# A third landing tile for the q and k loads, with the mask setup's tiles moved into a weight block's place

## Chip, cores, metric

The kernel runs on one NeuronCore of one Trainium2 chip. Its metric is device time in microseconds (us) of one execution, the median of three. Five engines run side by side, each through its own instruction stream in a fixed order: PE (TensorE, matmuls), DVE (VectorE), ACT (ScalarE), POOL (GpSimd) and SP (SyncE, which here only starts transfers). They wait for one another through semaphores. Transfers between device memory and the on-chip memory (SBUF) are started from SP and from ACT.

## The reference, cut to what matters

```python
# attention: batch 4, heads 8, sequence 768, head size 64; 4 sink columns, window 128
scores = q @ k^T / sqrt(64)
keep   = (pos_k < n_sink) | ((0 <= pos_q - pos_k) & (pos_q - pos_k < window))
a      = softmax(where(keep, scores, -1e9))
x      = (a @ v), heads side by side        # 3072 tokens x 512
# feed-forward
h = x @ w_in                                # 512 -> 2048
g = max(h, 0) + alpha * min(h, 0)
out = g @ w_out                             # 2048 -> 512
```

All of it is float32 at the interface.

## The kernel before

**Tiling.** The 3072 tokens are cut into 12 chunks `c` of 256 queries. For a chunk, `attention(c)` goes over 8 heads; each head has two units of 128 queries (`unit`), which see only a window of 260 keys and sinks. Then come the transposition of the weights and the product with v (`av_split`, `av`, `av_two`), which leaves the chunk's x as a rounded part `xh` and a remainder `xl`. The feed-forward part takes 16 weight blocks `f` of 128 hidden units: `gemm1(c, f)` makes h on PE (L863), ACT and DVE make g and its two parts `gh` and `gl` (L867 to L870), and `gemm2(c, f)` adds their product to the chunk's output (L898 to L901).

**Loads of the heads.** One transfer brings q and k of a head (`load_head`, L441) into a tile of the kind `stage`, 128 x 648 floats (324 KB); there are two such tiles. For the chunks 0 and 1 (`SPLIT`) one transfer brings a pair of heads, and PE reads the tile itself (L585), so it comes free when the second unit of the pair is done. From chunk 2 on ACT and DVE make a rounded copy `kq` of it (`prep_head`: L558 and L559 on ACT, L560 and L562 on DVE), and the tile comes free with L562. `next_load()` places the load of a later head in the program wherever a head begins. The first chunk's four pairs do not use `stage`: they land in `early`, tiles lent from places of SBUF that weight blocks 15 and 14 will take much later (`lend`; the tag `w15`, `w14`). The first values v land in the place of block 13 the same way.

**Weights.** A weight block arrives as 1 MB of raw 64-bit numbers (`load_weights`, tile `wraw`) and is turned into a high and a low float32 part by `convert_weights`: L382 on ACT first, then DVE steps (L386, L387, L396), L401 on ACT or DVE and L404 on DVE. Blocks 0 to 3 are loaded from SP, 4 to 15 from ACT's queue (L372). A block may be loaded no sooner than the conversion of the block four before has begun.

**Mask setup.** In the first 6 us POOL and DVE build the masks of the window: index tiles `geo` and `geof`, 128 x 2 x 260 each (L503, L504), are written by POOL (L520 to L526) and read by DVE (L524 to L537). After that they are not used.

**What sets the order.** `Plan` is a list scheduler that runs while the program is built. Each step is an `op` with an engine, a cost in us from a small table and the values that it reads and writes; values of a kind (`stage`, `kq`, `wa`, PSUM banks and so on) share that kind's tiles in the order of their making. `draw` plays all engines forward with these costs, and `issue` writes each engine's instructions in the order found. It also keeps a model of the transfers: an op with `nbytes` is held back while the modelled transfer queue is more than `BACKLOG` = 4 us ahead. So a changed number of tiles can change the order on any engine. Up to 28 us, `fill` adds matmuls of no use (`idle`, L1057) where PE would stand still.

Of the kernel before, what the change touches and what calls it, by code (L numbers as in the profile page):

```python
# [9 lines left out]
F32 = mybir.dt.float32  # L10
# [5 lines left out]
I32 = mybir.dt.int32  # L16
# [3 lines left out]
P = 128  # L20
# [3 lines left out]
WIN = 2 * P + NS  # L24
QC = 2 * P
KC = 3 * P + 2 * NS
CPB = S // QC
NCHUNK = B * CPB
NF = DF // P
# [49 lines left out]
class Plan:  # L79
# [20 lines left out]
    def held(self, tile_):  # L100
        v = Value(None)
        v.at = tile_
        return v
# [218 lines left out]
def program(ctx, tc, qk, pairs, vp, vq, vs, w, par, out):  # L322
    nc = tc.nc
    const = ctx.enter_context(tc.tile_pool(name="const", bufs=1))
    fast = ctx.enter_context(ExitStack())
    pool = fast.enter_context(tc.tile_pool(name="main", bufs=1))
# [8 lines left out]
    def several(name, n, shape, dtype):  # L335
        plan.kind(name, [pool.tile(shape, dtype, name=f"{name}{i}") for i in range(n)])
# [2 lines left out]
    plan.kind("swap", [scratch.tile([4, P, P], F32, name=f"swap{i}") for i in range(2)])  # L339
    plan.kind("turns", [scratch.tile([4, P, 2 * 32], F32, name=f"turns{i}") for i in range(2)])  # L340
    trid = held(scratch.tile([P, 2, P], F32, name="trid"))
    several("stage", 2, [P, QC + KC], F32)
    several("kq", 2, [P, KC + 2 * QC], F32R)
    several("v", 2, [P, 3, 2, D], F32)
    several("pt_", 3, [P, 2, WIN], F32)
# [62 lines left out]
    stage, vtile, vst = {}, {}, {}  # L408

    lent = {}  # L410

    def lend(f, shape, count):
        box = {}

        def part(i):
            if "tile" not in box:
                box["tile"] = const.tile([P, count, *shape], F32, tag=f"w{f}", name="lent")
            return box["tile"][:, i]
        out_ = []
        for i in range(count):  # L420
            v = held(None)
            v.bind, v.box = lambda i=i: part(i), box
            out_.append(v)
        lent[f] = out_
        return out_

    early = lend(NF - 1, [QC + KC], 3) + lend(NF - 2, [QC + KC], 1)
    early_v = lend(NF - 3, [3, 2, D], 4)

    def bound(v):  # L430
# [38 lines left out]
    V = {}  # L469

    def setup(engine, cost, run, reads=(), writes=()):
        for x in (*reads, *writes):
            V.setdefault(x, held(x))
        return op(engine, cost, run, reads=[V[x] for x in reads], writes=[V[x] for x in writes])
# [26 lines left out]
    load_head(1, 1)  # L501
    load_head(1, 3)

    geo = pool.tile([P, 2, WIN], I32, name="geo")  # L504
    geof = pool.tile([P, 2, WIN], F32, name="geof")
    rel, relf = geo[:, 0, :2 * P], geof[:, 0, :2 * P]
    srel, srelf, past = [t.rearrange("p (a i s) -> p a i s", a=2, i=3) for t in (geo[:, 1, :6 * NS], geof[:, 1, :6 * NS], geof[:, 1, 6 * NS:12 * NS])]
    past = past[:, 0]
# [32 lines left out]
    setup("POOL", 0.3, lambda: nc.gpsimd.affine_select(tri[:, 1], tri[:, 1], pattern=[[1, P]], compare_op=ALU.is_ge, fill=0.0, base=0, channel_multiplier=-1), (), ("tri",))  # L541
    setup("DVE", 0.07, lambda: nc.vector.memset(fm, 0.0), (), ("fm",))

    xh, xl, prep, comb, sink, ptile_, sums, rinv, nms, wt = {}, {}, {}, {}, {}, {}, {}, {}, {}, {}

    def bank(c, n, tag):
# [528 lines left out]
    with tc.If(bad != 0):  # L1075
# [3 lines left out]
        with tc.For_i(0, B, 1) as b:  # L1079
            for cc in range(CPB):  # L1080
                x = general(nc, gen, ptile, cc, b, qk5, vp5, nsink, window, ident)
# [167 lines left out]
```

## Time and profile before

| | |
|---|---|
| median of 3 runs | 680.22 us (680.05 to 680.34) |
| the profiled execution | 680.29 us, of which the span from first to last instruction is 678.3 us |
| granted TensorE clock, mean | 0.995 |
| q and k loads (324 KB each) | 4 into lent tiles, 4 pairs and 80 heads into `stage` |
| weight loads (1 MB each) | 4 from SP, 12 from ACT |

The profile's views name a group of instructions by line, engine, operation and tiles (`pt<-pt,nm`: written tile, read tiles). "Busy" counts the time in which an engine works on an instruction. An idle stretch is put down to the event that ended it, its releaser: "<-DVE nm L607 1.2" reads "1.2 us of waiting, ended by line 607 on DVE". SPq and ACTq are the instructions that start transfers, and "to landing" is the time from a start to the moment at which the data may be used. Times within the profile are counted from the start of the span.

### The profile page before, as it was taken

How to read it: one execution, taken by the hardware profiler on the slowest of the kernel's cores; microseconds unless marked ns; L12 is line 12 of the kernel's file. 1: busy time of each engine (PE TensorE's matmuls, PEld its weight loads, DVE VectorE, ACT ScalarE, POOL GpSimd, SP SyncE). 2: the span in 40 equal slices, each digit the busy share in tenths (PEclk: the TensorE clock that was granted, in tenths of full speed). 3: DMA queues.
4: the chain of work that ended last, by engine and by line, in shares of the span. 5: the costliest groups of instructions: out<-in, count | busy, mean ns of one | idle time of the engine just before them, and what ended most of it. 6: DMA issues, size and time to landing. Idle time of an engine off the chain costs nothing.

```text
span 678.3 us, 13313 instructions
## 1 busy us (share of the span) xinstructions
PE 664.5 (98%) x4534; PEld 581.7 (86%) x4534; DVE 533.8 (79%) x1795; ACT 402.4 (59%) x1084; POOL 35.6 (5%) x115
## 2 busy tenths in 40 slices
PE   9989999999999999999999999999999999999996
PEld 4568898988889889898988988988988988988995
DVE  6999999968968967976986985895995995995331
ACT  6989987836637637536646545655654663743332
POOL 2110000001000000001000000000000000100000
PEclk9989999999999999999999999999999999999998
DMA  8765541434433544443443552543542453431001
GB/s 311 270 217 215 194 164 42 124 92 152 124 119 107 148 115 130 137 141 106 145 141 96 139 150 87 156 125 90 166 144 68 154 150 86 149 94 47 32 2 35
DMA packets 64732, 87.56 MB, mean 129 GB/s; under 512 B 13968, under 2 KB 41104, under 8 KB 64656
## 3 DMA queue, kind: packets, MB, share of 16 engines
q1 hardware_dynamic: 61104, 73.53, 36.0%
q10 hardware_dynamic: 3552, 13.11, 5.6%
q8 instruction: 37, 0.61, 0.4%
q14 instruction: 39, 0.32, 0.2%
HBM read 68.40 MB, written 18.22 MB: 128 GB/s over the span
## 4 chain that ended last, share of the span: by engine, by line
PE 82%; DVE 9%; ACT 5%; issue 2%; DMA 2%; POOL 0%; ACTq 0%; SPq 0%; DVEq 0%
PE bank L863 34%; PE bank L898 12%; PE bank L900 11%; PE bank L901 11%; PE bank L768 6%; PE bank L594 3%; PE bank L595 3%; DVE wa L396 2%; ACT pt L611 1%; DVE w L404 1%; DVE wa L394 1%; ACT wa L382 1%; DVE g L868 1%; DVE gl L870 1%; PE bank L838 1%
## 5 line engine op out<-in xcount | busy, mean ns | idle before, releaser
L863 PE MATMUL bank<-xh,w 128*128 128x256 f32 x1536 | 307.1, 281 | 1.5 <-DVE g L868 1.3
L863 PEld LDWEIGHTS bank<-xh,w 128*128 128x128 f32 x1536 | 251.1, 189 | 8.8 <-DVE g L868 1.8
L863 PE MATMUL bank<-xl,w 128*128 128x256 f32 x768 | 215.0, 280 | 0.0
L867 ACT ACTIVATE g<-bank,param 128x256 f32<-128x256 f32 x192 | 90.0, 471 | 114.9 <-PE bank L863 113.1
L900 PE MATMUL bank<-w,gh 128*128 128x512 f32 x382 | 151.9, 398 | 0.0
L901 PE MATMUL bank<-w,gh 128*128 128x512 f32 x382 | 149.9, 392 | 0.0
L863 PEld LDWEIGHTS bank<-xl,w 128*128 128x128 f32 x768 | 145.0, 189 | 5.2
L869 ACT CAST gh<-g 128x256 fp32r<-128x256 f32 x192 | 77.4, 404 | 89.0 <-DVE g L868 88.8
L868 DVE TENSOR_TENSOR g<-bank,g 128x256 f32<-128x256 f32 x192 | 80.1, 418 | 62.9 <-ACT g L867 62.5
L898 PE MATMUL bank<-w,gl 128*128 128x512 f32 x382 | 120.4, 397 | 0.0
L611 ACT ACTIVATE pt<-pt,nm 128x260 f32<-128x260 f32 (+1 forms) x192 | 94.2, 491 | 28.6 <-DVE nm L607 27.4
L870 DVE TENSOR_TENSOR gl<-g,gh 128x256 fp32r<-128x256 f32 x192 | 80.7, 422 | 25.0 <-ACT gh L869 22.0
L607 DVE CUSTOM_DVE_ANT_0 pt<-bank,masks 128x260 f32<-128x260 f32 (+1 forms) x192 | 74.5, 399 | 12.6 <-PE bank L595 9.1
L898 PEld LDWEIGHTS bank<-w,gl 128*128 128x128 f32 x382 | 69.5, 188 | 16.0 <-issue 2.2
L900 PEld LDWEIGHTS bank<-w,gh 128*128 128x128 f32 x382 | 71.9, 188 | 8.4 <-ACT kq L558 0.2
L901 PEld LDWEIGHTS bank<-w,gh 128*128 128x128 f32 x382 | 71.9, 188 | 8.4
L752 DVE TENSOR_TENSOR wa<-comb,tri 128x256 f32<-128x256 f32 x144 | 51.4, 419 | 2.1 <-DMA comb<-swap 1.9
L560 DVE TENSOR_TENSOR kq<-stage,kq 64x392 fp32r<-64x392 f32 x80 | 45.3, 566 | 5.7 <-ACT kq L558 3.3
L656 POOL TENSOR_TENSOR sink<-pt,ri 128x8 f32<-128x8 f32 x80 | 22.4, 280 | 494.4 <-DVE ri L641 205.3
L558 ACT CAST kq<-stage 128x392 fp32r<-128x392 f32 x80 | 41.4, 517 | 11.0 <-PE bank L595 6.3
L594 PE MATMUL bank<-kq 128*128 128x260 f32 (+1 forms) x160 | 45.2, 283 | 1.0 <-DVE nm L607 0.8
L595 PE MATMUL bank<-kq 128*128 128x260 f32 (+1 forms) x160 | 45.0, 281 | 0.1
(126 smaller groups left out, 685.6 us busy)
## 6 DMA issues: line engine op xcount, KB each, us to landing
stage<-qk SPq DMA_DIRECT2D x80, 324.0 KB, 3.0
wraw<-w ACTq DMA_DIRECT2D x12, 1024.0 KB, 5.3
swap<-comb SPq DMA_DIRECT2D x36, 256.0 KB, 2.0
comb<-swap SPq DMA_DIRECT2D x36, 256.0 KB, 3.1
v<-vq SPq DMA_DIRECT2D x36, 192.0 KB, 2.5
out_dram<-ob SPq DMA_DIRECT2D x22, 256.0 KB, 2.2
wraw<-w SPq DMA_DIRECT2D x4, 1024.0 KB, 12.3
turns<-comb SPq DMA_DIRECT2D x18, 128.0 KB, 3.3
```

Source lines behind the costliest of these rows:

```text
L594: nc.tensor.matmul(s[:, w0], qh()[:, qs], ks()[:, kw], start=True, stop=False)
L595: nc.tensor.matmul(s[:, w0], ql()[:, qs], ks()[:, kw], start=False, stop=True)
L607: op("DVE", dve(n), lambda: nc.vector.tensor_tensor_reduce(out=pt.at[:, u, w0], in0=s.at[:, w0], in1=masks[:, i, w0], scale=-0.125, scalar ...
L611: op("ACT", exp(n), lambda: nc.scalar.activation(pt.at[:, u, w0], pt.at[:, u, w0], AF.Exp, bias=nm.at[:, h, u:u + 1], scale=-1.0, accum_ou ...
L863: nc.tensor.matmul(h(), fin.at[:, 0, part, ks], rhs.at[:, kt], start=(kt == 0 and n == 0), stop=(kt == KT - 1 and n == 2))
L867: op("ACT", act(QC, True), lambda: nc.scalar.activation(g.at, h(), AF.Copy, scale=alt[:, f:f + 1]), reads=[bk, known("param")], writes=[g])
L868: op("DVE", dve(QC), lambda: nc.vector.tensor_tensor(g.at, h(), g.at, ALU.max), reads=[bk], writes=[g])
L869: op("ACT", cast(QC), lambda: nc.scalar.copy(gh.at, g.at), reads=[g], writes=[gh])
L870: op("DVE", dve(QC), lambda: nc.vector.tensor_tensor(gl.at, g.at, gh.at.bitcast(F32), ALU.subtract), reads=[g, gh], writes=[gl])
L898: nc.tensor.matmul(o2[j].at, gl.at[:, js], fin.at[:, 1, 0], start=False, stop=(f == NF - 1))
L900: nc.tensor.matmul(o2[j].at, gh.at[:, js], fin.at[:, 1, 0], start=(f == 0), stop=False)
L901: nc.tensor.matmul(o2[j].at, gh.at[:, js], fin.at[:, 1, 1], start=False, stop=False)
```

## The change

`stage` has three tiles in place of two. `geo` and `geof` are no tiles of their own any more: they lie behind the fourth early pair in the tile that is lent from weight block 14's place. The load of block 14 has the five mask values in the list of things that it must wait for.

```diff
-    several("stage", 2, [P, QC + KC], F32)
+    several("stage", 3, [P, QC + KC], F32)
...
     early = lend(NF - 1, [QC + KC], 3) + lend(NF - 2, [QC + KC], 1)
+    shared = const.tile([P, 1, QC + KC + 4 * WIN], F32, tag=f"w{NF - 2}", name="lent")
+    early[3].box["tile"] = shared[:, :, :QC + KC]
     early_v = lend(NF - 3, [3, 2, D], 4)
...
-    geo = pool.tile([P, 2, WIN], I32, name="geo")
-    geof = pool.tile([P, 2, WIN], F32, name="geof")
+    spare = shared[:, 0, QC + KC:].rearrange("p (n a x) -> p n a x", n=2, a=2)
+    geo, geof = spare[:, 0].bitcast(I32), spare[:, 1]
...
+    lent[NF - 2] += [V[x] for x in ("rel", "srel", "relf", "srelf", "past")]
```

The diff puts three lines in, so that a line number behind them is 2 or 3 higher after the change (L441 becomes L443, L607 becomes L610, L863 becomes L866). What it does to the order of the instructions shows at three places.

**SP, some 11 to 40 us into the span.** The rows start transfers; a name's first number is the buffer (`stage0`, `stage1`, `stage2`), and `pairs` and `qk` are the loads of two heads and of one. Before:

```order
L372 DMA wraw_324<-w 128x2x1024
L456 DMA v0_83<-vp 128x384
L456 DMA v1_84<-vp 128x384
L710 DMA trid_78<-tri_133 128x256
L441 DMA stage0_79<-pairs 128x648
L441 DMA stage1_80<-pairs 128x648
L441 DMA stage0_79<-qk 128x648
L456 DMA v0_83<-vp 128x384
```

After:

```order
L372 DMA wraw_323<-w 128x2x1024
L443 DMA stage2_81<-pairs 128x648
L458 DMA v0_84<-vp 128x384
L458 DMA v1_85<-vp 128x384
L713 DMA trid_78<-tri_133 128x256
L443 DMA stage0_79<-pairs 128x648
L443 DMA stage1_80<-qk 128x648
L443 DMA stage2_81<-qk 128x648
L458 DMA v0_84<-vp 128x384
```

The third pair of chunk 1 moves up behind weight block 3 and ahead of the first v loads. From there on each slot of a `stage` load stays where it was in SP's order and carries the next pair or head. The pattern holds to the last chunk, in which one slot is left over and falls away.

**ACT, 25 to 38 us.** `wraw` with a new number each time is weight block 4, 5, 6 (`wraw_380`, `432`, `472` before; `430`, `470`, `479` after), and the last row of each piece is the first step on block 4. Before:

```order
L707 CAST sinkT0_108<-bank2_66 128x256
L372 DMA wraw_380<-w 128x2x1024
L401 CAST w1_383<-wa1_93 128x2x512
...
L611 ACTIVATE pt_0_85,sm1_99<-pt_0_85,nm1_97 128x260
L372 DMA wraw_432<-w 128x2x1024
L635 COPY comb0_88<-bank2_66 128x512
...
L372 DMA wraw_472<-w 128x2x1024
L611 ACTIVATE pt_1_86,sm1_99<-pt_1_86,nm1_97 128x260
L611 ACTIVATE pt_2_87,sm1_99<-pt_2_87,nm1_97 128x260
L382 ACTIVATE wa0_92,size_124<-wraw_380 128x1024
```

After:

```order
L614 ACTIVATE pt_0_86,sm1_100<-pt_0_86,nm1_98 128x260
L372 DMA wraw_430<-w 128x2x1024
L638 COPY comb0_89<-bank2_66 128x512
...
L372 DMA wraw_470<-w 128x2x1024
L614 ACTIVATE pt_1_87,sm1_100<-pt_1_87,nm1_98 128x260
L614 ACTIVATE pt_2_88,sm1_100<-pt_2_88,nm1_98 128x260
L372 DMA wraw_479<-w 128x2x1024
L382 ACTIVATE wa0_93,size_125<-wraw_430 128x1024
```

The first of the three starts falls away; block 4 starts in the slot that block 5 had, block 5 in that of block 6, and block 6 directly ahead of the first step on block 4. All of ACT's other rows up to the last chunk's attention are in the order that they had.

**PE and DVE, in the last chunk's attention (near 600 us).** PE's score products (L594, L595, from then L597, L598) of one unit move from behind the ninth of a block's twelve `gemm1` products to ahead of the first. On DVE, before:

```order
L870 TENSOR_TENSOR gl2_123<-g1_117,gh2_120 128x256
L560 TENSOR_TENSOR kq1_82<-stage1_80,kq1_82 64x392
L752 TENSOR_TENSOR wa1_93<-comb1_89,tri_133 128x256 x4
L562 TENSOR_TENSOR kq1_82<-stage1_80,kq1_82 128x256
L868 TENSOR_TENSOR g0_116<-bank4_68,g0_116 128x256
L607 ISA pt_0_85,nm1_97<-bank0_64,masks_131 128x260
```

After:

```order
L873 TENSOR_TENSOR gl2_124<-g1_118,gh2_121 128x256
L610 ISA pt_0_86,nm1_98<-bank0_64,masks_131 128x260
L755 TENSOR_TENSOR wa1_94<-comb1_90,tri_133 128x256 x4
L563 TENSOR_TENSOR kq1_83<-stage2_81,kq1_83 64x392
L565 TENSOR_TENSOR kq1_83<-stage2_81,kq1_83 128x256
L871 TENSOR_TENSOR g0_117<-bank4_68,g0_117 128x256
```

One evacuation of a score bank (L607) moves four rows up, and two more steps of the same chunk change places behind it. Outside of these few dozen rows PE, DVE and POOL run the same instructions in the same order before and after.

## The prediction

> **What bounds the kernel now.** I read the page's first part, then the busy time by stretch, then who PE waits for.
>
> ```profile
> PE 664.5 (98%) x4534; PEld 581.7 (86%) x4534; DVE 533.8 (79%) x1795; ACT 402.4 (59%) x1084; POOL 35.6 (5%) x115
> ...
> 20.00:130.00 110.00, 105.65 (x696) 88.95 (x696) 107.48 (x254) 96.53 (x220) 6.39 (x17) 0.98 0.52 174
> 130.00:620.00 490.00, 488.29 (x3399) 437.39 (x3400) 396.87 (x1445) 274.91 (x790) 24.77 (x76) 1.00 0.42 124
> ```
>
> The two rows of stretches give, behind the length, the busy us of PE, PE's weight loads, DVE, ACT and POOL, then the granted clock, the share of the transfer engines and GB/s. There are two regimes. From 20 to 130 us, while weights are converted, DVE is busy 107.48 of 110 us: it leaves 110 - 107.48 = 2.5 us in which it could go faster. From 130 to 620 us PE is busy 488.3 of 490 us, and its order and number of matmuls are the kernel's arithmetic. The whole span's DVE share of 79% is a mean over both and hides the first.
>
> A third tile for loads can only help where something waits for a load. PE's longest waits and the only one on a transfer, and then what stood ahead of the engines when they turned to a `stage` tile (any access to it, PE, ACT or DVE):
>
> ```profile
> PE bank L585 <- DVE nm L607: 2.2, 2, 1.2
> PE bank L863 <- DVE g L868: 1.3, 2, 0.7
> ...
> PE bank L594 <- DVE nm L607: 0.8, 1, 0.8
> ...
> PE bank L585 <- DMA lent<-pairs: 0.3, 1, 0.3
> ...
> its engine sat idle before it (us, times) until:
>   PE bank L595: 6.3, 16
>   DVE nm L607: 4.9, 4
>   ACT kq L558: 3.3, 12
>   ACT xh L848: 3.2, 6
>   issue: 1.1, 4
>   ACT gh L869: 1.0, 5
> ```
>
> Each row is waiter, releaser, us in total, times, longest (the second list: releaser, us, times). The only load that PE waited for is that of a lent tile at the start, 0.3 us, and that load is the same after the change. In the second list every releaser is an engine; no transfer is among them. So the loads into the two tiles are always there in time already.
>
> How early they are is seen best where they are tightest, in the start, when weights fill the queues:
>
> ```profile
> 28.89 0.33 SPq L441 DMA_DIRECT2D stage<-pairs  x1
> stage<-pairs SPq DMA_DIRECT2D x1, 324.0 KB, 2.9
> 34.07 0.33 SPq L441 DMA_DIRECT2D stage<-pairs  x1
> 35.80 1.05 PE L585 MATMUL bank<-stage 64*128 64x260 f32 x4 [1.21 <-DVE nm L607]
> ```
>
> The load of chunk 1's third pair starts at 28.89 and lands 2.9 us later (the row of transfers for that start), at 31.8; PE reads it at 35.80, 4.0 us after. The 1.21 us ahead of that matmul are a score bank's, not the load's.
>
> **The loads after the change, step by step.** In SP's order every `stage` slot stays, from 28.89 us on, and carries the next load. Before, the load of head m waits until head m-2 has left its tile (two tiles). After, that slot loads head m+1 into the third tile on, so it waits for head m+1-3 = m-2: the same event. SP is therefore held as long as before at each slot, and the transfers that transpose the attention weights (`swap`, `comb`, `turns`) and v loads queued behind it on SP start when they did. Their bytes are the same at the same times. 80 heads and 4 pairs are loaded in either case. Gain: 0 us, because a load that is a head earlier replaces one that nobody waited for. Where the last slot falls away, near 590 us, the transfer behind it on SP can start a little sooner; PE waits for none of these in that stretch, so 0 us too.
>
> The one extra early load: the third pair goes out at the place of the first v load, in a stretch with full transfer engines.
>
> ```profile
> 12.15 1.38 SPq L456 DMA_DIRECT2D v<-vp  x2
> 10.00:20.00 10.00, 9.42 (x63) 5.07 (x61) 8.41 (x25) 9.37 (x27) 1.48 (x4) 1.00 1.04 403
> 23.00:26.00 3.00, 2.85 (x19) 1.77 (x18) 2.85 (x7) 2.94 (x8) 1.04 (x2) 1.00 0.16 59
> v<-vp SPq DMA_DIRECT2D x1, 192.0 KB, 12.6
> 43.55 1.63 PE L768 MATMUL bank<-comb,v 128*64 128x256 f32 x18
> ```
>
> At 403 GB/s its 324 KB (331,776 bytes) take 0.82 us. Weight block 3 is ahead of it in the queue and does not move. The two v loads and the mask transfer behind it land 0.82 us later; v landed at 12.15 + 12.6 = 24.8 and is read at 43.55, so 18 us cover it. The backlog runs into the nearly empty 23 to 26 us (share 0.16). Cost: 0; without that cover it would be 0.82 us.
>
> **The weight loads on ACT** are the only part with a thin cover.
>
> ```profile
> 25.36 0.44 ACTq L372 DMA_DIRECT2D wraw<-w  x1
> 30.00 0.39 ACTq L372 DMA_DIRECT2D wraw<-w  x1
> 33.69 0.37 ACTq L372 DMA_DIRECT2D wraw<-w  x1
> 37.26 1.13 ACT L382 ACTIVATE wa<-wraw 128x1024 f32<-128x1024 f32 x1 [0.38 <-DVE w L404]
> 44.73 1.17 ACT L382 ACTIVATE wa<-wraw 128x1024 f32<-128x1024 f32 x1
> ...
> wraw<-w ACTq DMA_DIRECT2D x1, 1024.0 KB, 5.0
> wraw<-w ACTq DMA_DIRECT2D x1, 1024.0 KB, 6.1
> wraw<-w ACTq DMA_DIRECT2D x1, 1024.0 KB, 5.6
> DMA to landing us min/median/max: 4.8/5.8/13.2
> ```
>
> The first three rows are the starts of blocks 4, 5 and 6, the next two ACT's first steps on blocks 4 and 5; then the three blocks' times to landing in that order, and the spread over all 16 weight loads. After the change block 4 starts where block 5 did, at 30.00. Block 5's row is the measurement of that slot, with the same load from SP (28.89) just ahead of it: 6.1 us, so block 4 lands at 36.1. ACT turns to it at 37.26. **The cover shrinks from 37.26 - 30.4 = 6.9 us to 1.2 us, and holds.** Block 5 starts at 33.69 and lands near 39.3 (5.6 us), 5.4 us ahead of its step at 44.73. Block 6 starts just ahead of 37.26 and lands near 43.4 (6.1 us), and ACT's step on it comes later still than that on block 5. What the start itself costs ACT is bounded by its row of 0.44 us: that much could be won at 25.36, and 0.44 - 0.38 = 0.06 us lost ahead of 37.26, where ACT idles 0.38 us. Both lie in the stretch that DVE sets, so I take 0.
>
> Why block 5 took 6.1 us and block 4 only 5.0: the Trainium skill, page "DMA: Bandwidth & Descriptors", section "Queues, rings and completion order", says that each transfer engine takes turns between the queues of SP and ACT, and that a completion signal lands only after all earlier writes of that engine, in any queue. By it a weight load behind an SP load of 324 KB ends up to 0.8 us later, as an estimate from that page and the rate of 403 GB/s; the trace's difference of 1.1 us is near it. As block 4's new slot is measured with that neighbour, the sum by the rule is the same; it says only that a further SP load in front would eat most of the cover.
>
> **The mask tiles** cost nothing: same POOL and DVE instructions in the same order with the same tiles waited for, done by 5.4 us, while block 14's load starts at 86.98:
>
> ```profile
> 4.35 1.07 DVE L537 TENSOR_SCALAR masks<-geof,pv 128x128 bf16<-128x128 f32 x5
> 86.98 0.37 ACTq L372 DMA_DIRECT2D wraw<-w  x1
> ```
>
> **The last chunk's reordering.**
>
> ```profile
> 600.16 0.28 PE L863 MATMUL bank<-xh,w 128*128 128x256 f32 x1
> 601.22 0.28 PE L594 MATMUL bank<-kq 128*128 128x260 f32 x1
> 598.59 1.43 DVE L752 TENSOR_TENSOR wa<-comb,tri 128x256 f32<-128x256 f32 x4
> 600.61 0.42 DVE L607 CUSTOM_DVE_ANT_0 pt<-bank,masks 128x260 f32<-128x260 f32 x1
> ```
>
> The score products of 601.22 go to 600.16. They need the score bank that the evacuation of 600.61 frees; that now comes ahead of the four mask products of 598.59 and is over by 598.59 + 0.42 = 599.0, so PE finds the bank free more than 1 us before. DVE's steps on g behind it move back by one or two evacuations, at most 2 x 0.42 = 0.8 us. `gemm2` uses them two blocks later (`LAG`), a dozen products and more. Cost 0; 0.8 us if that cover were gone.
>
> **The sum**: 0 + 0 + 0 + 0 on the profiled execution's 680.29 us, which lies 0.07 above the median of 680.22. Forecast 680.2.
>
> **Rivals.**
>
> *Slower: block 4 comes too late.* ACT runs in order, so if the load takes longer than 37.26 - 30.00 = 7.3 us, all behind L382 slips: the copies that feed PE's products, and through them DVE, in the stretch where DVE has 2.5 us of slack in 110. The price is the time to landing less 7.3 us; with the longest landing among the weight rows, 13.2 us, it is 5.9 us: 686.1. For it speaks that this cover is the thinnest and that rows of 12 to 13 us exist. Against it: those are SP's loads under the full queue of the first 23 us, and from 25 us on the three rows are 5.0 to 6.1. It needs 8.7 us or more to show at 0.2%. The clock could add to it:
>
> ```profile
> 34.00:39.00 5.00, 2.76 (x15) 1.84 (x16) 4.81 (x16) 4.24 (x11) 0.96 (x2) 1.00 0.97 346
> 39.00:44.00 5.00, 4.99 (x27) 4.33 (x27) 4.94 (x11) 5.00 (x15) 1.09 (x2) 0.66 0.27 72
> ```
>
> After a stretch with PE busy 2.76 of 5 us the granted clock is 0.66, and PE is then busy throughout. The Trainium skill, page "TensorE: Matmul & The Clock Gate", section on the HAM clock gate, has the clock halved after an idle window of about 3.4 us; the trace agrees in kind. By it a late block would prolong the slow stretch by about one window, an estimate of 1.7 us more.
>
> *Faster: the loads did matter.* A wait for several things is put to the last; if the 2.2 us of L585 at 35.80 and 38.46 were the third pair's load in truth, they would go, with the dip of the clock behind them. 2.2 us off is 678.0, and DVE's 2.5 us is the most that can be had at all, 677.7. Against it: the load landed 4.0 us before, and DVE's bank evacuation ended right at the wait's end.
>
> *The cover at 600 us is missing*: 0.8 us, 681.0, still within 0.2%.
>
> **How the numbers follow.** 0.2% is 1.4 us, about what a measurement of this kernel can tell from no change. Forecast 0.86, and with the cover missing at 600 us 0.02, both within 0.2%; block 4 late by enough to show 0.07; faster 0.05. Within the forecast, PE's two waits after 130 us (0.8 and 0.7 us, the row of L594, and the longest in that of L863) hang on small shifts of DVE and may go or grow: about 0.8 either way, and the 0.8 upwards from the last chunk is no more than that. So 679.4 to 681.1 holds more than 8 in 10; the rivals' ends lie outside.
>
> **What would show it.** Right: in the profile after, no transfer among the releasers at `stage`; starts of `stage` loads at the same times as before from 28.9 us on; ACT's L382 at 37.3 without a wait on `wraw`; block 4's load started near 30.0 and landed by 36.2; the same waits of PE. Wrong: a wait of ACT for `wraw<-w` near 37 us, more idle DVE than 2.5 us up to 130 us, a longer dip of the clock, or a wait of DVE for `comb<-swap` that grew from the loads' new neighbours.

## The result, and the profile after

| | before | after |
|---|---|---|
| median | 680.13 us (679.99 to 680.34) | 683.9 us (683.67 to 684.3) |
| after / before, 95% interval | | 1.0056 [1.0044, 1.0069] |
| profiled execution, span | 680.29, 678.3 us | 683.68, 682.0 us |
| PE busy in the span | 664.5 us | 669.7 us |

The kernel is 3.8 us slower, and PE is busy 5.2 us longer with the same matmuls. The profile after, its busy line and the busy time by stretch (behind the length: PE, PE's weight loads, DVE, ACT, POOL, then granted clock, transfer share, GB/s):

```profile
PE 669.7 (98%) x4532; PEld 583.8 (86%) x4534; DVE 534.1 (78%) x1795; ACT 404.8 (59%) x1084; POOL 36.2 (5%) x115
```

```profile
39.00:44.00 5.00, 4.99 (x48) 4.05 (x46) 4.93 (x11) 5.00 (x16) 1.08 (x2) 1.00 0.74 293
...
130.00:620.00 490.00, 489.13 (x3374) 436.58 (x3373) 394.58 (x1437) 275.27 (x785) 25.05 (x76) 1.00 0.41 123
```

The last row is the one to read beside the prediction's. In the same 490 us, at the same clock of 1.00, PE was busy 488.29 us with 3399 matmuls before and is busy 489.13 us with 3374 now: 143.7 ns for one before, 145.0 ns after. PE has no new gap; it gets 25 fewer matmuls done in a stretch in which it never rests, and 25 x 145 ns are 3.6 us. The first row shows that the loss comes in spite of a better start: there the granted clock was 0.66 before and is 1.00 now, and at 65 us the steps that make g start 0.84 us earlier than before. From about 100 us on the lead melts away evenly. The better start is not the change's doing. Among the kernels tried below, e2 has three `stage` tiles and e6 has two, and in this stretch they show, in this order:

```profile
39.00:44.00 5.00, 4.99 (x29) 4.31 (x29) 4.95 (x11) 5.00 (x16) 1.10 (x2) 0.66 0.66 263
```

```profile
39.00:44.00 5.00, 4.99 (x48) 4.00 (x46) 4.94 (x11) 5.00 (x16) 1.09 (x2) 1.00 0.25 70
```

The same in steps from one matmul's start to the next one's, averaged over all neighbours within a product between 160 and 590 us, without the slowest twentieth: 116.0 ns before and 118.0 after in the first product (L863 before, L866 after), 230.7 and 232.7 in the second. Times the matmuls in 130 to 620 us (1763 and 882 before) that is 1763 x 2.0 + 882 x 2.05 ns = 5.3 us. Less the 0.84 us of the better start, and less 0.8 us because PE's wait at L594 (near 443 us) is gone, this is about the 3.7 us between the spans.

What the prediction had looked at is as it said. Who PE waits for now, and what stood ahead of the engines when they turned to a `stage` tile:

```profile
PE bank L588 <- DVE nm L610: 2.2, 2, 1.2
PE bank L866 <- DVE g L871: 1.2, 2, 0.7
PE bank L1060 <- DVE fm L544: 1.0, 1, 1.0
PE bank L633 <- ACT pt L614: 0.7, 3, 0.3
PE bank L805 <- ACT sinkT L710: 0.6, 1, 0.6
```

```profile
its engine sat idle before it (us, times) until:
  PE bank L598: 5.8, 15
  DVE nm L610: 5.2, 5
  ACT xh L851: 3.9, 7
  ACT kq L561: 3.5, 15
  ACT gh L872: 1.4, 5
  issue: 0.7, 3
```

No load is among them, and no wait has grown by what the kernel lost. At the start, weight block 4's load and ACT's first step on it:

```profile
30.23 0.43 ACTq L372 DMA_DIRECT2D wraw<-w  x1
...
37.49 1.12 ACT L382 ACTIVATE wa<-wraw 128x1024 f32<-128x1024 f32 x1 [0.39 <-DVE w L404]
```

```profile
wraw<-w ACTq DMA_DIRECT2D x1, 1024.0 KB, 5.5
```

The load starts at 30.23 and lands at 35.7, 1.8 us ahead of the step at 37.49, which waited only for DVE.

So the same instructions of one engine became longer. The diff does one thing that the prediction passed over: the third tile takes 648 x 4 = 2592 bytes in each partition ahead of all tiles that follow in the code, and these move up by 2592 bytes. The weights do not move (but for blocks 0, 14 and 15). The addresses of PE's operands in the built programs, in bytes within a partition, and the remainders that they leave on division by 256:

| | before | after |
|---|---|---|
| weight blocks 1 to 13 | from 42016 to 140320, 8192 apart: remainder 32 | the same |
| xh, xl (4096 bytes each) | from 195808: remainder 224 | from 198400: remainder 0 |
| gh, gl (1024 bytes each) | from 214240: remainder 224 | from 216832: remainder 0 |
| distance to the weights, by its remainder on division by 256 | 192 | 224 |

### The profile page after: what moved, and what is told of

Same layout as the page of the kernel before. It is cut to its first block, busy times and chain, and to the rows that moved or that the text cites. A ratio compares the mean times of both kernels' runs of the same rounds, so it can differ in the third digit from the quotient of the medians.

```text
span 682.0 us, 13314 instructions
## 1 busy us (share of the span) xinstructions
PE 669.7 (98%) x4532; PEld 583.8 (86%) x4534; DVE 534.1 (78%) x1795; ACT 404.8 (59%) x1084; POOL 36.2 (5%) x115
## 4 chain that ended last, share of the span: by engine, by line
PE 88%; DVE 5%; ACT 4%; issue 1%; POOL 0%; ACTq 0%
PE bank L866 38%; PE bank L901 13%; PE bank L903 12%; PE bank L904 12%; PE bank L771 5%; PE bank L597 3%; PE bank L598 3%; DVE wa L396 1%; ACT pt L614 1%; DVE w L404 1%; ACT wa L382 1%; PE bank L1060 1%; PE bank L841 1%; ACT w L401 1%; DVE g L871 0%
## 5 line engine op out<-in xcount | busy, mean ns | idle before, releaser
L866 PE MATMUL bank<-xh,w 128*128 128x256 f32 x1536 | 310.0, 282 | 1.2 <-DVE g L871 1.2
L866 PEld LDWEIGHTS bank<-xh,w 128*128 128x128 f32 x1536 | 250.9, 188 | 8.8 <-DVE g L871 1.8
L866 PE MATMUL bank<-xl,w 128*128 128x256 f32 x768 | 216.0, 281 | 0.0
L866 PEld LDWEIGHTS bank<-xl,w 128*128 128x128 f32 x768 | 144.5, 188 | 5.3
L873 DVE TENSOR_TENSOR gl<-g,gh 128x256 fp32r<-128x256 f32 x192 | 80.9, 423 | 25.1 <-ACT gh L872 22.2
L610 DVE CUSTOM_DVE_ANT_0 pt<-bank,masks 128x260 f32<-128x260 f32 (+1 forms) x192 | 74.9, 400 | 13.7 <-PE bank L598 9.3
L598 PE MATMUL bank<-kq 128*128 128x260 f32 (+1 forms) x160 | 45.1, 282 | 0.1
L597 PE MATMUL bank<-kq 128*128 128x260 f32 (+1 forms) x160 | 44.7, 280 | 0.1
```

Of the source, the lines that this page charges most:

```text
L597: nc.tensor.matmul(s[:, w0], qh()[:, qs], ks()[:, kw], start=True, stop=False)
L598: nc.tensor.matmul(s[:, w0], ql()[:, qs], ks()[:, kw], start=False, stop=True)
L610: op("DVE", dve(n), lambda: nc.vector.tensor_tensor_reduce(out=pt.at[:, u, w0], in0=s.at[:, w0], in1=masks[:, i, w0], scale=-0.125, scalar ...
L866: nc.tensor.matmul(h(), fin.at[:, 0, part, ks], rhs.at[:, kt], start=(kt == 0 and n == 0), stop=(kt == KT - 1 and n == 2))
L873: op("DVE", dve(QC), lambda: nc.vector.tensor_tensor(gl.at, g.at, gh.at.bitcast(F32), ALU.subtract), reads=[g, gh], writes=[gl])
```

## The experiments

Two theories at first. PLACE: the matmuls take longer because their operands lie elsewhere. LOADS: the third tile, its earlier loads or the order that follows slow PE. In the diffs "idle" tiles are used by nothing. The order of the matmuls is that of before in the kernels built on before and in e1, and that of after in all others.

### Addresses or loads

Four kernels: two `stage` tiles with the addresses of after; three with the addresses of before; the kernel before moved by 32 bytes; the kernel after moved on to 4096 bytes above before.

```diff
# e1, against after
-    several("stage", 3, [P, QC + KC], F32)
+    several("stage", 2, [P, QC + KC], F32)
+    pool.tile([P, QC + KC], F32, name="idle_a")
# e2, against after
-    several("stage", 3, [P, QC + KC], F32)
+    stages = [pool.tile([P, QC + KC], F32, name=f"stage{i}") for i in range(2)]
...
     several("gl", LAG + 1, [P, QC], F32R)
+    plan.kind("stage", stages + [pool.tile([P, QC + KC], F32, name="stage2")])
# e3, against before
     several("stage", 2, [P, QC + KC], F32)
+    pool.tile([P, 8], F32, name="idle_a")
# e4, against after
     several("stage", 3, [P, QC + KC], F32)
+    pool.tile([P, 376], F32, name="idle_a")
```

> The kernel after with two stage tiles, and in the third one's room a tile of the same size that nothing uses. Loads and the order on PE, ACT and SP are those of before; the addresses of all tiles are those of after (kq to gl 2592 bytes per partition higher than before). Theory PLACE (PE's matmuls take some ns longer because their operands lie elsewhere in SBUF): 683.9 us, xl products about 118.5 ns from start to start instead of 116. Theory LOADS (the third tile, its earlier loads and the order that follows from it slow PE): 680.1 us and 116 ns.

> The kernel after, with the third stage tile put behind gl instead of behind the second. Loads and the order on every engine are those of after; kq to gl have the addresses of before. PLACE: 680.1 us and 116 ns from start to start of the xl products. LOADS: 683.9 us and 118.5 ns.

> The kernel before with a 32-byte tile that nothing uses behind the stage tiles: kq to gl lie 32 bytes higher. Their addresses then leave the same remainder on division by 512 as those of after (2592 = 5 x 512 + 32). PLACE, if only the alignment to 64, 128, 256 or 512 bytes matters: 683.9 us. PLACE, if larger distances matter, and LOADS: 680.1 us.

> The kernel after with a 1504-byte tile that nothing uses behind the third stage tile: kq to gl lie 4096 bytes higher than before. Loads and order are those of after. PLACE, if the address matters only by its remainder on division by some power of two up to 4096: 680.1 us. PLACE by the distance itself: neither 680.1 nor 683.9 for sure. LOADS: 683.9 us.

All kernels are set side by side here; the distances are those of xh, xl and of gh, gl to the weights by the remainder on division by 256, and "first" and "second" the mean ns from start to start in the two products, found as above. A ratio compares runs of one session on one chip; the sessions are several, so it is not the quotient of two medians of this table.

| kernel | distances | median us | to before, 95% | first | second |
|---|---|---|---|---|---|
| before | 192, 192 | 680.1 | | 116.0 | 230.7 |
| after | 224, 224 | 683.9 | 1.0056 [1.0044, 1.0069] | 118.0 | 232.7 |
| e1 two tiles, places of after | 224, 224 | 684.4 | 1.0072 [1.0059, 1.0086] | 118.0 | 232.8 |
| e2 third tile last | 192, 192 | 679.5 | 0.9992 [0.9983, 1.0001] | 115.9 | 230.9 |
| e3 before, 32 bytes | 224, 224 | 684.4 | 1.0072 [1.0058, 1.0086] | 118.0 | 232.7 |
| e4 after, 4096 bytes | 192, 192 | 679.3 | 0.9988 [0.9979, 0.9997] | 115.9 | 230.9 |
| e5 before, 64 bytes | 0, 0 | 686.1 | 1.0089 [1.0073, 1.0104] | 119.2 | 231.6 |
| e6 only g, gh, gl | 192, 224 | 683.2 | 1.0049 [1.0035, 1.0063] | 116.7 | 233.0 |
| e7 only xh, xl by 32 | 224, 0 | 684.0 | 1.0055 [1.0041, 1.0069] | 118.2 | 231.3 |
| e8 all tiles by 32 | 192, 192 | 679.6 | 0.9992 [0.9983, 1.0001] | 116.0 | 230.7 |
| e9 | 160, 160 | 685.4 | 1.0071 [1.0049, 1.0094] | 117.9 | 233.2 |
| e10 | 128, 128 | 685.0 | 1.0073 [1.0051, 1.0095] | 118.6 | 231.8 |
| e11 | 64, 64 | 684.1 | 1.0062 [1.0040, 1.0085] | 117.5 | 233.4 |
| e12 (448 of 512) | 192, 192 | 680.1 | 0.9999 [0.9987, 1.0011] | 115.9 | 230.9 |
| e14 | 112, 192 | 682.0 | 1.0031 [1.0019, 1.0042] | 117.7 | 230.8 |
| e15 | 192, 240 | 679.3 | 0.9991 [0.9981, 1.0001] | 116.1 | 229.9 |
| e16 | 112, 240 | 681.5 | 1.0028 [1.0017, 1.0039] | 117.5 | 231.1 |

e1 and e2 decide. The stretch 130 to 620 us of e1, and then of e2:

```profile
130.00:620.00 490.00, 489.13 (x3376) 436.79 (x3376) 395.06 (x1437) 275.31 (x787) 24.77 (x76) 1.00 0.41 123
```

```profile
130.00:620.00 490.00, 489.12 (x3403) 437.79 (x3402) 396.79 (x1446) 275.60 (x790) 25.03 (x76) 1.00 0.42 123
```

Two tiles at the addresses of after do 3376 matmuls, as after; three tiles at the addresses of before do 3403, as before. LOADS falls. 32 bytes alone make the kernel before as slow as the change does (e3), and 4096 bytes bring it back (e4): the address counts by a remainder.

### Which remainder, which operand, and to what

e5 and e8 move all of kq to gl by 64 bytes and every tile, the weights too, by 32; e6 and e7 move only the second product's operands, or mainly the first's.

```diff
# e5, against before
     several("stage", 2, [P, QC + KC], F32)
+    pool.tile([P, 16], F32, name="idle_a")
# e6, against before
+    pool.tile([P, 8], F32, name="idle_a")
     several("g", 2, [P, QC], F32)
# e7, against before
+    pool.tile([P, 8], F32, name="idle_a")
     several("xh", 2, [P, KT, QC], F32R)
...
+    pool.tile([P, 8], F32, name="idle_b")
     several("g", 2, [P, QC], F32)
# e8, against before
     const = ctx.enter_context(tc.tile_pool(name="const", bufs=1))
+    const.tile([P, 8], F32, name="idle_a")
```

> The kernel before with a 64-byte idle tile behind the stage tiles: kq to gl lie 64 bytes higher. If the remainder on division by 64 decides (32 in the fast kernels so far, 0 in the slow ones): 680.0 us. If the remainder on division by 128 or more decides: another time, 684 us where 128 is the period and 96 the only good one.

> The kernel before with a 32-byte idle tile ahead of g: only g, gh and gl lie 32 bytes higher, at a multiple of 64. Theory MOVING (the tiles that stream through PE in the first product, xh and xl, must not lie there): 680.0 us. Theory STATIONARY (gh and gl, which PE loads as weights in the second product): 684.4 us. Each costs its own products: about 681.6 us, by the share of the second product in PE's growth between before and after (2.2 of 6 us).

> The kernel before with 32 idle bytes ahead of xh and 32 more ahead of g: xh and xl lie 32 bytes higher, at a multiple of 64, and g, gh and gl 64 bytes higher, at the old remainder. MOVING: 684.4 us. STATIONARY: 680.0 us. Each costs its own products: about 682.8 us. Neither of the two (the cause is in the tiles from kq to ob): 680.0 us here and in the run with g, gh and gl.

> The kernel before with a 32-byte idle tile ahead of all others: every tile, the weights with them, lies 32 bytes higher. If the place of PE's two operands to each other decides (weights and xh, xl, gh, gl leave the same remainder of 64 in the fast kernels and different ones in the slow): 680.0 us, as nothing moved against anything. If a multiple of 64 is bad in itself: 684.4 us, or more, since the weights now lie there too.

My guess that multiples of 64 are bad was wrong: 64 bytes are worse than 32 (686.1 us). e8 says why. Like e3 it puts xh, xl, gh and gl at multiples of 64, and yet it is as fast as before; its stretch row:

```profile
130.00:620.00 490.00, 488.57 (x3403) 437.45 (x3403) 396.36 (x1444) 274.79 (x788) 24.92 (x76) 1.00 0.42 124
```

So it is the **distance between the operand tiles and the weights**, not an address by itself. e6 and e7 show that each product answers mainly to its own operands: moving g, gh and gl raises the second product by 2.3 ns and the first by 0.7; moving xh and xl by 32 raises the first by 2.2. In the first product xh and xl stream through PE while weights are loaded; in the second the weights stream and gh, gl are loaded. Both pairings feel the distance. e7 also moved gh and gl to a distance of 0, which I had taken for harmless; that is 0.6 ns of its second product. Both kernels came out slower than "each costs its own products" had it (683.2 against 681.6 us, 684.0 against 682.8), and the 0.7 ns show that the first product is not independent of the second one's operands.

### All distances in steps of 32

The kernel after with 448, 416, 352 and 736 idle bytes behind the third tile (the diff of e4 with other sizes).

> The kernel after (three stage tiles) with 448 idle bytes behind them: kq to gl lie 3040 bytes above before, and xh, xl, gh, gl begin 160 bytes above the weights by the remainder of 512 (before 192; after and the run with 32 bytes 224; the run with 64 bytes 256). Theory DISTANCE with period 256 (PE reads its two operands at once, the moving one and the next one's weights, and is held up the more, the nearer they come): 160 is farther from 256 than 192, so faster than before, about 677 us and 115 ns from start to start in the first product. DISTANCE with period 128: 160 is 32, which no run has shown; the time stays open. No law in the distance: anything from 676 to 686 us.

> As the last, with 416 idle bytes: distance 128. DISTANCE with period 256: the farthest point, the fastest of all, about 675 us and 113 to 114 ns throughout. DISTANCE with period 128: as with 64 bytes on the kernel before (256), 686 us and 119.5 ns.

> As the last, with 352 idle bytes: distance 64. DISTANCE with period 256, the same on both sides: 64 is as far from 0 as 192 from 256, so 680 us and 116 ns. With period 128: 64 is 192, so 680 us too. If the side matters (which operand runs ahead): another time.

> As the last, with 736 idle bytes: distance 448, which is 192 + 256. Period 256 or 128: 680 us and 116 ns, as before. Period 512: another time, and by the nearness to 512 as at 64.

A period of 256 fits: 448 is like 192 in every column, while 64, which would equal 192 at a period of 128, is slow. 448 is the only distance above 256 that was tried. The rest of my law fell: 128 and 160 should have been the fastest and are among the slowest. Of the six distances tried by then only 192 is good, and the kernel before happened to have it in both products.

### PE alone

Is it PE's own two reads, or a neighbour's access? A kernel with nothing but such matmuls, on 16 operand tiles at distances of 0 to 240, alone and then beside DVE and ACT:

```diff
+    for d in x:
+        for o, l, r, s, t in first(d, 6):
+            nc.tensor.matmul(o, l, r, start=s, stop=t)
+        for o, l, r, s, t in second(d, 12):
+            nc.tensor.matmul(o, l, r, start=s, stop=t)
...
+    for i in range(360):
+        nc.scalar.copy(e, a)
+        nc.vector.tensor_tensor(c, a, b, ALU.subtract)
+    for d in range(0, 256, 32):
+        for o, l, r, s, t in first(d, 6):
+            nc.tensor.matmul(o, l, r, start=s, stop=t)
...
```

> A kernel that leaves everything out but the two products' matmuls: one weight tile and 16 operand tiles d000x to d240x, named by how many bytes above the weights they begin by the remainder of 256. For each of them 72 matmuls as in the first product (the operand tile streams, 256 columns) and 72 as in the second (the operand tile is loaded as weights, the weight tile streams, 512 columns). First all 16 with no other engine at work, then the eight multiples of 32 beside a stream of DVE subtractions and ACT copies on other tiles; its output is not the reference's. Theory READS (PE's own two reads disturb one another, and the distance sets how much): already alone, d192x takes about 116 ns from start to start in the first product and about 231 in the second, and the others 118 to 120 and 234. Theory OTHERS (a neighbour's access, by DVE, ACT or a transfer, disturbs PE): alone all are equal within 0.5 ns, and the differences come in the second half, if at all. If all are equal in both halves, the distance works only together with something that this kernel leaves out.

Its busy time by stretch shows that in the first half nothing but PE worked, at full clock, and that DVE and ACT were busy beside it in the second:

```profile
50.00:350.00 300.00, 300.00 (x1715) 262.03 (x1714) 0.00 (x0) 0.00 (x0) 0.00 (x0) 1.00 0.00 1
430.00:595.00 165.00, 165.00 (x957) 144.80 (x956) 152.65 (x360) 145.87 (x359) 0.00 (x0) 1.00 0.00 1
```

Then the first product's line, alone: duration min/median/max in ns, first and last start in us.

```profile
L83 PE MATMUL bank<-d000x,weights x72: 283/283/284, 25.2 to 33.7; 128*128 128x256 f32 x72
...
L83 PE MATMUL bank<-d112x,weights x72: 274/275/283, 202.1 to 210.2; 128*128 128x256 f32 x72
...
L83 PE MATMUL bank<-d192x,weights x72: 281/281/283, 328.4 to 336.8; 128*128 128x256 f32 x72
```

From first to last start are 71 steps: 8.5 us at distance 0, 8.1 at 112. From the single records the means are 113.8 ns at 112, 116.6 to 117.7 at 32, 64, 192 and 240, and 118.1 to 120.0 at the others, 0 among them; in the second product 226.8 at 0 and 240, 229.7 at 176, and 231.7 to 233.9 at all others. READS had the distances wrong: 192 was to be the fastest, at about 116 and 231 ns, and takes 117.7 and 233.3. Its core is shown: **PE alone is slowed by the distance of its own two operands.** Beside DVE and ACT nothing changed at the six distances from 0 to 160 (0.1 ns or less).

At 192, in the second half, the first product went from 117.7 to 113.4 ns and the second from 233.3 to 228.7. DVE and ACT are not what holds it there: ACT's stream had ended by 588 us and DVE's by 595.3, while this second product runs from 588.9 to 605.1 us. Its last part has no neighbour:

```profile
596.00:605.00 9.00, 9.00 (x41) 7.40 (x40) 0.00 (x0) 0.00 (x0) 0.00 (x0) 1.00 0.00 0
```

Its steps take 228.9 ns in the mean before DVE's end and 228.9 after it. The matmuls ahead of this block are others than in the first half (distance 160 in place of 176).

### Do the distances that are fast alone help the kernel?

Three whole kernels with three `stage` tiles, where xh, xl lie at 112, or gh, gl at 240, or both, and one more with matmuls alone in three other orders.

```diff
# e14, against after (e15 does the same with gh and gl, e16 both)
     several("stage", 3, [P, QC + KC], F32)
+    pool.tile([P, 120], F32, name="idle_a")
...
-    several("xh", 2, [P, KT, QC], F32R)
-    several("xl", 2, [P, KT, QC], F32R)
+    pool.tile([P, 40], F32, name="idle_b")
+    wide = pool.tile([P, 4 * KT * QC + 4], F32R, name="x")
+    four = [wide[:, 4 + i * KT * QC:4 + (i + 1) * KT * QC].rearrange("p (k n) -> p k n", k=KT) for i in range(4)]
+    plan.kind("xh", four[:2])
+    plan.kind("xl", four[2:])
+    pool.tile([P, 16], F32, name="idle_c")
# m2: the loops over x reversed; with a matmul of 64 columns between groups; and in turns
+        for m in range(6):
+            for o, l, r, s, t in one[12 * m:12 * m + 12]:
+                nc.tensor.matmul(o, l, r, start=s, stop=t)
+            for o, l, r, s, t in two[6 * m:6 * m + 6]:
+                nc.tensor.matmul(o, l, r, start=s, stop=t)
```

> The kernel after with three stage tiles; kq to ob and g, gh, gl at the distances of before (192 for g, gh, gl), xh and xl in one tile at distance 112 from the weights by the remainder of 256. If the intervals of the run with matmuls alone hold in the whole kernel: 114.1 ns in the first product in place of 116.2, on about 1720 matmuls between 130 and 620 us, so 3.6 us less than before: 676.4 us. If the distance gives only which intervals are possible and the neighbours in PE's stream choose among them: between 680 and 685 us, as at all other distances but 192.

> The kernel after with three stage tiles; kq to xl at the distances of before (192 for xh, xl), gh and gl in one tile at distance 240. If the intervals with matmuls alone hold: 227.1 ns in the second product in place of 231.5, on about 860 matmuls, so 3.8 us less than before: 676.2 us. If the neighbours choose: 680 to 683.5 us, since moving gh and gl alone by 32 bytes gave 683.2.

> Both of the last two: xh, xl at 112 and gh, gl at 240. If the intervals with matmuls alone hold: 680 - 3.6 - 3.8 = 672.6 us. If the neighbours choose: 684 us or more.

> As the run with matmuls alone (all else left out, its output is not the reference's), nothing beside PE, and each of the 16 distances three times: the same blocks with the distances in reversed order; the same with one short matmul of 64 columns between groups; and the two products in turns, 12 and 6 matmuls, as in the kernel. If the distance alone sets the interval: each distance has the same mean in all three and in the run before (112: 114.1; 192: 117.8 as without DVE and ACT). If each distance has several possible intervals and what goes before chooses: means that differ by 3 to 5 ns between the three, 192 between 113.7 and 117.8, as the two halves of the run before had it, and the order by distance changes.

The gain of 112 did not come: the first product takes 117.7 ns in the kernel, not 114. With 240 for gh and gl the second product is a little faster (229.9), the time the same. Both at once give 681.5 us, neither the 672.6 nor the 684 or more that was expected. The last run shows why 112 fails. Its first rows are the blocks in reversed order, and then, in a fence of their own, the two products in turns as in the kernel (first and last start enclose five blocks of the second product too):

```profile
L82 PE MATMUL bank<-d192x,weights x48: 281/281/283, 75.6 to 81.2; 128*128 128x256 f32 x48
...
L82 PE MATMUL bank<-d112x,weights x48: 275/275/282, 159.9 to 165.2; 128*128 128x256 f32 x48
```

```profile
L98 PE MATMUL bank<-d000x,weights x72: 277/283/363, 585.2 to 600.7; 128*128 128x256 f32 x72
...
L98 PE MATMUL bank<-d112x,weights x72: 275/281/287, 703.6 to 719.0; 128*128 128x256 f32 x72
...
L98 PE MATMUL bank<-d192x,weights x72: 276/276/285, 788.3 to 803.3; 128*128 128x256 f32 x72
...
L98 PE MATMUL bank<-d240x,weights x72: 277/280/283, 838.6 to 853.8; 128*128 128x256 f32 x72
```

In reversed order the first product gives the numbers of the run before within 0.4 ns (112: 113.9), except 118.4 at 128. In turns 112 loses its lead, and 192 is the fastest of all: 15.0 us from first to last start against 15.2 to 15.5. At 192, from the second block of the first product on, the first five of twelve steps take 116 to 122 ns and the other seven 113 or 114: both intervals occur at one distance, with no other engine at work. Set beside the whole kernels:

| distance | 192 | 64 | 112 | 160 | 224 | 128 | 0 |
|---|---|---|---|---|---|---|---|
| PE alone, in turns, first product, ns | 115.2 | 117.7 | 118.0 | 118.4 | 118.1 | 119.1 | 119.3 |
| whole kernel, first product, ns | 116.0 | 117.5 | 117.7 | 117.9 | 118.0 | 118.6 | 119.2 |

With matmuls alone in the kernel's order the whole kernel's figures for the first product come out within 0.8 ns and nearly in the same order. The weights leave a remainder of 128 in that run and of 32 in the kernels, so here too it is the distance and not the address. In the second product the two agree within 0.7 ns at 0, 64, 128, 160, 224 and 240, but at 192 matmuls alone take 228.5 ns and the kernel 230.7. **Distance and the order of PE's stream together set the interval; no other engine is needed for the differences.** With a short matmul between groups the step right behind it takes 195 to 205 ns; the others take 116.6 ns (at 192, again the fastest) to 119.7, and 112 has no lead there either (118.5).

No version beats the kernel before by as much as 0.2%: the best ratio is e4's, 679.3 us, 0.9988 [0.9979, 0.9997], and e8, which moved no tile against another, gave 0.9992.

## Why the prediction was wrong, step by step

Forecast 680.2, range 679.4 to 681.1, 0.88 for no change; it came out 683.9.

- *Nobody waits for the `stage` loads, so a third tile gains nothing*: right. With the addresses held, three tiles give 0.9992, 0.9988 and 0.9999 (e2, e4, e12). Their intervals reach from 0.9979 to 1.0011, so at most some 0.2% can hide there.
- *SP's slots stay, the extra early load is covered*: right. The `stage` loads that started at 28.89, 34.07 and 39.54 us start at 29.12, 34.35 and 39.76; the third pair now starts at 11.73 and lands at 25.1, and nothing waits for a load.
- *The weight loads' cover shrinks from 6.9 to 1.2 us, and holds*: right in kind, 1.8 us. The rival built on it (686.1) did not happen.
- *The last chunk's order costs 0*: the waits of PE show nothing that grew there.
- *The mask tiles "cost nothing: same POOL and DVE instructions in the same order with the same tiles waited for"*: right. e2 has them where the change puts them and is as fast as before.
- *"Gain: 0 us" for the third tile, and no other term for it*: **here the sum failed.** It counted the tile's loads and put its room at nothing without a reason. That room lies ahead of PE's operands in the order of allocation, and these moved up by 2592 bytes. The tile without that shift (e2) takes 679.5 us, the shift without the tile (e1) 684.4.
- *"From 130 to 620 us PE is busy 488.3 of 490 us, and its order and number of matmuls are the kernel's arithmetic"*: order and number, yes; I read that as if their time were fixed too, and **that is the second half of the failure**. A matmul's time rose by 1.7% in the first product and 0.9% in the second. PE has only 1.7 us of slack in these 490, so nearly every ns showed: 5.3 us. No term, rival or bound stood for the length of an unchanged instruction, so the range was too narrow for what it left out.
- *A longer dip of the clock* was named as a sign of being wrong. In the profiled execution there was none (1.00 in place of 0.66 from 39 to 44 us), which hid some 0.8 us of the loss there. That was luck: e1, at the addresses of after, shows 0.66 in this stretch, e2 with three tiles 0.66 and e6 with two tiles 1.00. What sets the dip is not shown.

The Trainium skill, page "TensorE: Matmul & The Clock Gate", section "Step-by-step: what each phase is for", says that PE has two independent read ports into SBUF and that loading the next weights takes no read bandwidth from the running matmul. By that one would not expect the distance to matter. The runs differ: PE alone at full clock takes 113.8 to 120.0 ns for the same matmul by the distance of its operands. The measurement decides.

What stays open is what in the chip does it. Two reads meeting in one part of the memory would fit a period of 256 bytes, but no run shows the memory itself; my simple form of it, slower the nearer, was refuted by 128 and 160. Nor is it known why 192 has two intervals (117.7 and 113.4 ns) with the same operands, or what makes PE pass from one to the other. Weight blocks 14, 15 and 0 lie elsewhere in the kernels built on after; block 14, alone with another remainder (192 in place of 32), was not tried by itself, but e2, e4 and e12 have it there too and lose nothing.

## What to carry to other kernels

A change that adds, removes or resizes an on-chip tile can move every tile that is allocated behind it; where PE is the bound, list the addresses of its operands before and after, and keep their distance to the weights (here by its remainder on division by 256), or take the tile from the end of the pool. If a kernel slows evenly while no wait grows, compare the number of matmuls in the same stretch at the same clock: it shows longer instructions at once. A good distance found with matmuls alone holds only if they stand in the kernel's own order.

## What the hardware showed that was not expected

- 32 idle bytes ahead of PE's operands cost 4.4 us of 680 (1.0072 [1.0058, 1.0086]).
- The same matmul of 256 columns starts every 113.8 to 120.0 ns, and that of 512 columns every 226.8 to 233.9 ns, by the distance of its two operands, with no other engine at work.
- In the whole kernel, steps of 114 ns or less are 36% of the first product's before (distance 192) and 1% after (224), and steps of 120 to 123 ns are 5% before and 30% after: the mean moves because a faster kind of step vanishes and a slower one appears, not because each grows a little.
